# Attention scores of two key-tile pairs issued together as 64-row products

## The chip, the cores and the metric

The kernel runs on one core of a Trainium2 chip. The metric is the device time of one execution in microseconds, inputs and outputs in the chip's memory; the median of several executions is compared.

## The reference

There are 8 batches of 3136 tokens, a model width of 256, and a score width of 64. First comes an attention without softmax whose keys and queries are the same matrix, then a feed-forward block for the 128 tokens of each batch that score highest on a gate.

```python
scores = (1.0 / S) * np.matmul(z, z.transpose(0, 2, 1))      # z: 8 x 3136 x 64
attn = np.maximum(scores, 0.0) ** 2
x = u * np.matmul(attn, v)                                   # u, v: 8 x 3136 x 256
...
s = np.einsum('bsd,d->bs', x, w_gate)
top = np.argpartition(-s[b], capacity)[:capacity]            # capacity 128
h = np.maximum(x[b, top] @ w1, 0.0)
out[b, top] = x[b, top] + sigmoid(s[b, top]) * (h @ w2)      # w1: 256 x 1024, w2: 1024 x 256
```

All is float32. The scores are symmetric, since `z` stands on both sides.

## The kernel before

**Split operands.** Each float32 operand of the large products is split into a high part that TensorE's `float32r` type holds and a low part, the rest. `ZH` and `ZL` hold the two parts of the transposed `z` (64 rows), and each of the two tiles holds its 64 rows twice: in partitions 0 to 63 and again in 64 to 127. For a chunk of queries, `Z[b, c]` has the high part in rows 0 to 63 and the low part in rows 64 to 127. A product of 128 rows with `ZH` as the stationary operand therefore gives high by high plus high by low, and one with `ZL` gives low by high plus low by low: two matmuls for a key tile and a chunk of queries.

**Tiling.** The queries of a batch go in seven chunks (`CHUNKS`): five whole ones of 512 columns (`WHOLE` = 5), then one of 256 and one of 320. The keys go in 24 tiles of 128 and one half tile of 64. A slot (`slots`) is one chunk with two key tiles, or with the half tile; a chunk has 13 slots, twelve pairs and the half tile last. A pair is "old" (`is_old`) if its squared scores were already worked out for an earlier chunk as the other half of the symmetric matrix: they were transposed on VectorE (L453), stored to memory, and are fetched and only split again. Chunk `c` of the whole ones has 2c old pairs and 12 - 2c new ones; the chunks of 256 and 320 columns have 10 old and 2 new.

**Order of the slots.** Old and new pairs of a chunk are spread evenly over it by sorting on `(i + 0.5) / len`. The second new pair of a whole chunk (`is_second`, not in the very first chunk) works on 256 columns only, since the rest is the transpose of the first (`is_first`), and is put next to last among the new ones.

**One slot.** `mix(k)` issues the 12 products of a pair into two accumulators (L520): eight of the high part `hi` by `V`'s high and low part, then four of the low part `lo`. After the eighth it calls `between`, which issues the scores of slot k + 3 (`LEAD` = 3) by `scores(k)`. For a new pair that is four products into one of two score buffers (pool `ps_s`, `bufs=2`, each of two PSUM banks, one for each key tile of the pair), then on ScalarE a Relu (L424) and a Square that writes `hi` (L425), then on VectorE the product L435 of score and Relu, or on ScalarE a Square (L430), as a list of expected loads (`busy`) decides. `settle_scores` then issues L435 and `low`: the low part `lo` (L484, on GpSimd or VectorE), the transposes and the stores. A score buffer is free again when L435, or L424 where L430 is used, has read it.

**Other work.** TensorE executes in the order of the program, and each engine's order is written out by hand. Loads, splits of the next batch's `z` and `v`, fetches of old pairs and the routing are planned by slot number (`at_slot`) and run between the slots: routing multiplies with small stationary tiles (L721, L761, L771, L772, L844), spread over the slots of the next batch.

Of the kernel before, what the change touches and what calls it, by code (L numbers as in the profile page):

```python
# [10 lines left out]
F32 = mybir.dt.float32  # L11
# [7 lines left out]
P = 128  # L19
CH = 512  # L20
# [11 lines left out]
def chunks_of(S):  # L32

    n = (S - CH) // CH
    half = CH // 2
    rest = S - n * CH - half
    assert rest % Q == 0 and half <= rest <= CH
    return [(i * CH, CH) for i in range(n)] + [(n * CH, half), (n * CH + half, rest)]
# [46 lines left out]
def attention_then_routed_ffn(ctx: ExitStack, tc: tile.TileContext, zt, ut, v, wg, w1, w2, cst, cst16, keys, outs, at, cap):  # L85
    nc = tc.nc
# [4 lines left out]
    CHUNKS = chunks_of(S)  # L91
    NCH = len(CHUNKS)
    WHOLE = NCH - 2
# [16 lines left out]
    ps_s = ctx.enter_context(tc.tile_pool(name="ps_s", bufs=2, space=bass.MemoryType.PSUM))  # L110
# [76 lines left out]
    for o in range(0, W, 2 * D):  # L187
        kk, f = divmod(o, F)
# [6 lines left out]
    ZH = const.tile([P, S + 64], F32R, name="ZH")  # L195
    ZL = const.tile([P, S + 64], F32R, name="ZL")
# [3 lines left out]
    def by_rows(z, c0, n):  # L200

        g = c0 // CH * CH
        rows = slice((c0 - g) // P, (c0 - g + n) // P)
        return z[:, g : g + CH].rearrange("p (t f a) -> p f t a", t=GT, a=Q)[:, rows]

    Z = {}
# [97 lines left out]


    slots = []
    for b in range(B):
        for c in range(NCH):
            old = [(2 * g, 2 * g + 1) for g in range(min(c, WHOLE) * GT // 2)]
            new = [(2 * g, 2 * g + 1) for g in range(min(c, WHOLE) * GT // 2, NJ // 2)]  # L310
            if c < WHOLE and (b or c):

                new.insert(len(new) - 2, new.pop(1))
            both = [((i + 0.5) / len(old), 0, js, True) for i, js in enumerate(old)]
            both += [((i + 0.5) / len(new), 1, js, False) for i, js in enumerate(new)]
            slots += [(b, c, js, is_old) for _, _, js, is_old in sorted(both)]
            slots.append((b, c, (NJ,), False))
    assert len(slots) == B * NCH * SLOTS

# [16 lines left out]
    def is_second(k):  # L336

        b, c, js, _ = slots[k]
        return (b or c) and c < WHOLE and js[0] == c * GT + 2
# [6 lines left out]
    def spend(act=0.0, dve=0.0, pool=0.0):  # L346
        busy["act"] += act
        busy["dve"] += dve
        busy["pool"] += pool
# [35 lines left out]
    def old_scores(k):  # L385
        b, c, js, _ = slots[k]
        w = CHUNKS[c][1]
        g, t = js[0] // GT, js[0] % GT
        src = fetched[b, c, g][:, :, t * Q : (t + 2) * Q].rearrange("p f (q a) -> p q f a", a=Q)
        hi = work.tile([P, 2, CH], F32R, name="hi", tag="hi2", bufs=LEAD)[:, :, :w]  # L390
        by = lambda x: x.rearrange("p q (f a) -> p q f a", a=Q)
        nc.scalar.copy(by(hi), src)  # L392
        spend(act=0.15 + 0.00167 * w)
        lows.append((k, src, hi, [(by, src)], lambda: None))

    def turns(k):
        b, c, js, _ = slots[k]
        return c < WHOLE and js[0] * P >= CHUNKS[c][0] + CH

    def scores(k):  # L400
        b, c, js, is_old = slots[k]
        if is_old:
            return old_scores(k)
        n = len(js)
        c0, w = CHUNKS[c]
        mov = Z[b, c]
        if is_second(k):
            mov, w = mov.rearrange("p (f x) -> p f x", x=P)[:, :, P // 2 :], w // 2
        ps = ps_s.tile([P, 2, CH], F32, name="sc", tag="sc")[:, :, :w]
        todo = [(q, j, z) for q, j in enumerate(js) for z in (ZH, ZL)]  # L410
        if k < 2:
            todo.sort(key=lambda x: x[2] is ZL)
        for q, j, z in todo:
            nc.tensor.matmul(ps[:, q], z[:, j * P : (j + 1) * P], mov, start=z is ZH, stop=z is ZL)  # L414
        a = work.tile([P, 2, CH], F32, name="a", tag="a")[:, :n, :w]
        hi = work.tile([P, 2, CH], F32R, name="hi", tag="hi2", bufs=LEAD)[:, :n, : CHUNKS[c][1]]
        pieces = [(lambda x: x, a)]
        if is_second(k):
            by = lambda x: x.rearrange("p q (f x) -> p q f x", x=P)
            pieces = [(lambda x: by(x)[..., 64:], a.rearrange("p q (f x) -> p q f x", x=64))]  # L420
            pieces.append((lambda x: by(x)[..., :64], fetched[b, c, c].rearrange("p f (q x) -> p q f x", q=2)))
        act, dve = 0.13 + 0.0008 * w * n, 0.15 + 0.00104 * w * n
        turned = 0.16 + 0.00118 * w * n if turns(k) else 0.0
        nc.scalar.activation(a, ps[:, :n], AF.Relu)  # L424
        nc.scalar.activation(pieces[0][0](hi), pieces[0][1], AF.Square)  # L425
        for view, src in pieces[1:]:
            nc.scalar.copy(view(hi), src)
            spend(act=act)
        if n == 2 and busy["act"] + 3 * act < busy["dve"] + dve + turned:
            nc.scalar.activation(a, a, AF.Square)  # L430
            square = lambda: None
            spend(act=3 * act)
        else:
            rows = slice(0, P) if n == 2 else slice(64, P)
            square = lambda: nc.vector.tensor_tensor(a[rows], ps[rows, :n], a[rows], op=ALU.mult)  # L435
            spend(act=2 * act, dve=dve)
        lows.append((k, a, hi, pieces, square))
# [95 lines left out]
    rows = {}  # L533
# [590 lines left out]
    for b in range(B):  # L1124
        k0 = b * per

        for i in range(NCH):
            if b == 0:
                k = (0, 0, 0, 1, 3, 5, 6)[i]
            elif i < WHOLE:  # L1130
                k = k0 - per + (i + 1) * SLOTS + 7
            else:
                k = k0 - 1 + 4 * (i - WHOLE)
# [9 lines left out]
        for g in range(NJ // 2 + 1):  # L1143
            k = k0 - 10 + 3 * g // 2 if b else max(1, g - 2)
# [20 lines left out]
    for (b, c, g), ks in used.items():  # L1165
        k = max(ks[0] - AHEAD, room.popleft() - LEAD + 2)
# [6 lines left out]
    for i, (load, use) in enumerate(weight_tasks):  # L1173
        k = (1 + i // 4) * SLOTS
# [19 lines left out]
    def more_scores(upto):  # L1194
        nonlocal issued
        while issued <= min(upto, len(slots) - 1):
            scores(issued)
            issued += 1
# [199 lines left out]
```

## Time and profile before

| | |
|---|---|
| Median of 3 runs | 2113.93 us (2113.89 to 2115.18) |
| The profiled execution, and its span | 2112.39 us, 2110.6 us |
| Granted TensorE clock, mean | 0.998 |
| Busy share: PE, PEld, DVE, ACT, POOL | 99%, 83%, 72%, 60%, 64% |
| Matmuls, weight loads | 10583, 10583 |
| Chain by line, the two largest | PE acc L520 68%, PE sc L414 13% |

PE is TensorE's matmuls and PEld its weight loads, DVE is VectorE, ACT is ScalarE, POOL is GpSimd. The span runs from the first to the last instruction; the execution's time is a little longer. In a group of the profile, the shape `128*128 128x512` is a stationary tile of 128 rows and 128 columns and a moving operand of 128 rows and 512 columns. A matmul's own duration is a model, and matmuls overlap: what one costs is read from the start of one to the start of the next. In a timeline row the first number is the start in microseconds from the span's start, the second the time from the first start to the last end of the instructions merged in it; in brackets stands the idle time ahead of it, with what ended it. A row of waits has the work waited for, the microseconds in all, and how often.

### The profile page before, as it was taken

The page shows a single profiled execution, that of the slowest core. Times are in us where ns is not written, and L with a number is a line of the kernel's source. Part 1 is how long each engine was busy: PE and PEld are TensorE (multiplying, and loading weights), DVE is VectorE, ACT ScalarE, POOL GpSimd, SP SyncE. Part 2 cuts the span into 40 slices and gives each one's busy share as a digit, 9 for nine tenths or more (in the row PEclk, how much of TensorE's full clock was granted, in tenths as well). Part 3 has the DMA queues.
Part 4 walks back from the last instruction along what each step waited for, and adds up shares of the span by engine and source line. Part 5 has one row for each costly group of instructions (what it writes and reads, how often), then busy time and mean ns, then how long its engine had stood idle before and what let it go on. Part 6 is the DMA issues. An engine that isn't in the chain of part 4 may idle for free.

```text
span 2110.6 us, 31719 instructions
## 1 busy us (share of the span) xinstructions
PE 2091.1 (99%) x10583; PEld 1755.8 (83%) x10583; DVE 1529.9 (72%) x2304; ACT 1265.4 (60%) x1571; POOL 1347.7 (64%) x703
## 2 busy tenths in 40 slices
PE   8999999999999999999999999999999999999998
PEld 6788978889888898888988889888897888887788
DVE  8666678766777667776678766786667776787776
ACT  7565576545766457654676546765467654775543
POOL 6676577655766558765576655766567655666643
PEclk9999999999999999999999999999999999999999
DMA  6688766787667876678767787677775776665862
GB/s 187 198 250 231 201 187 172 187 231 215 180 185 183 230 206 188 190 187 226 212 185 190 185 225 209 187 199 184 208 229 174 196 189 169 201 186 160 215 175 93
DMA packets 425731, 412.03 MB, mean 195 GB/s; under 512 B 147616, under 2 KB 338912, under 8 KB 421984
## 3 DMA queue, kind: packets, MB, share of 16 engines
q1 hardware_dynamic: 424512, 407.66, 70.2%
q0 software_dynamic: 768, 2.10, 0.3%
q8 instruction: 83, 1.36, 0.3%
q14 instruction: 80, 0.66, 0.1%
q10 hardware_dynamic: 288, 0.26, 0.0%
HBM read 235.31 MB, written 172.23 MB: 193 GB/s over the span
## 4 chain that ended last, share of the span: by engine, by line
PE 83%; DMA 4%; DVE 4%; ACT 4%; issue 2%; POOL 2%; SPq 1%; POOLq 0%; DVEq 0%; ACTq 0%
PE acc L520 68%; PE sc L414 13%; DMA vst<-in_v 2%; ACT a L424 2%; POOL lo L484 1%; ACT hi L425 1%; DVE a L435 1%; DVE lo L484 1%; PE h L1038 1%; DMA squares<-aT 1%; DMA ut<-in_ut 0%; DMA qk<-squares_narrow 0%; PE y L1082 0%; DMA zst<-in_zt 0%; DVE ut L565 0%
## 5 line engine op out<-in xcount | busy, mean ns | idle before, releaser
L520 PE MATMUL acc<-hi,V 128*128 128x512 f32 (+2 forms) x5376 | 1230.6, 367 | 2.9 <-ACT hi L425 0.8
L484 POOL TENSOR_TENSOR lo<-a,hi 128x1024 fp32r<-128x1024 f32 (+2 forms) x327 | 756.5, 2316 | 609.5 <-DVE a L435 475.7
L520 PEld LDWEIGHTS acc<-hi,V 128*128 128x128 f32 x5376 | 932.5, 188 | 169.6 <-DVE ut L565 9.0
L520 PE MATMUL acc<-lo,V 128*128 128x512 f32 (+2 forms) x2688 | 666.2, 364 | 5.1 <-POOL lo L484 3.2
L424 ACT ACTIVATE a<-sc 128x1024 f32<-128x1024 f32 (+4 forms) x408 | 363.4, 891 | 507.1 <-PE sc L414 379.5
L520 PEld LDWEIGHTS acc<-lo,V 128*128 128x128 f32 x2688 | 473.8, 188 | 87.0 <-POOL lo L484 6.5
L435 DVE TENSOR_TENSOR a<-sc,a 128x1024 f32<-128x1024 f32 (+3 forms) x334 | 338.4, 1013 | 275.5 <-ACT hi L425 244.8
L392 ACT CAST hi<-qk 128x1024 fp32r<-128x1024 f32 (+2 forms) x320 | 275.0, 863 | 234.7 <-PE acc L520 205.2
L453 DVE STREAM_TRANSPOSE aT<-a 128x512 f32<-128x512 f32 (+1 forms) x520 | 340.9, 691 | 89.1 <-ACT a L430 61.9
L425 ACT ACTIVATE hi<-a 128x1024 fp32r<-128x1024 f32 (+4 forms) x408 | 377.4, 925 | 18.4 <-PE acc L520 1.1
L484 DVE TENSOR_TENSOR lo<-qk,hi 128x1024 fp32r<-128x1024 f32 (+2 forms) x223 | 308.9, 1393 | 66.5 <-ACT hi L392 63.4
L414 PE MATMUL sc<-Z,ZH 128*128 128x512 f32 (+2 forms) x760 | 281.4, 374 | 3.3 <-DVE a L435 2.2
L414 PE MATMUL sc<-Z,ZL 128*128 128x512 f32 (+2 forms) x760 | 278.7, 371 | 0.7 <-DVE ZL L120 0.7
L484 POOL TENSOR_TENSOR lo<-qk,hi 128x1024 fp32r<-128x1024 f32 (+2 forms) x97 | 190.3, 1964 | 56.9 <-ACT hi L392 37.8
L414 PEld LDWEIGHTS sc<-Z,ZH 128*128 128x128 f32 x760 | 142.9, 188 | 34.9 <-DVE a L435 8.0
L414 PEld LDWEIGHTS sc<-Z,ZL 128*128 128x128 f32 x760 | 142.9, 188 | 25.4 <-DVE ZL L120 1.1
L120 POOL TENSOR_TENSOR V<-vst,V 128x512 fp32r<-128x512 f32 x89 | 128.1, 1441 | 33.3 <-ACT V L119 33.0
L586 POOL TENSOR_TENSOR ut<-x,w_run 128x1024 f32<-128x1024 f32 (+2 forms) x52 | 127.0, 2442 | 23.3 <-DVE x L577 21.1
L119 ACT CAST V<-vst 128x512 fp32r<-128x512 f32 x95 | 57.8, 608 | 37.4 <-DMA vst<-in_v 37.4
L430 ACT ACTIVATE a<-a 128x1024 f32<-128x1024 f32 x74 | 78.6, 1062 | 2.3
L565 DVE SCALAR_TENSOR_TENSOR ut<-acc,ut 128x512 f32<-128x512 f32 (+2 forms) x112 | 64.0, 612 | 18.2 <-PE acc L520 17.9
L120 POOL TENSOR_TENSOR ZL<-zst,ZH 128x512 fp32r<-128x512 f32 (+2 forms) x56 | 73.6, 1320 | 3.0 <-DMA out<-x 2.2
(153 smaller groups left out, 1080.1 us busy)
## 6 DMA issues: line engine op xcount, KB each, us to landing
squares<-aT SPq DMA_DIRECT2D x160, 512.0 KB, 3.5
qk<-squares SPq DMA_DIRECT2D x320, 256.0 KB, 5.9
squares_narrow<-aT SPq DMA_DIRECT2D x320, 128.0 KB, 3.4
qk<-squares_narrow SPq DMA_DIRECT2D x80, 512.0 KB, 5.1
vst<-in_v SPq DMA_DIRECT2D x190, 128.0 KB, 3.2
out<-x SPq DMA_DIRECT2D x162, 128.0 KB, 3.3
ut<-in_ut SPq DMA_DIRECT2D x40, 512.0 KB, 4.6
squares_own<-aT SPq DMA_DIRECT2D x39, 256.0 KB, 2.1
```

Of the source, the lines that this page charges most:

```text
L120: (lo_on or nc.vector.tensor_tensor)(lo, src, hi.bitcast(F32), op=ALU.subtract)
L392: nc.scalar.copy(by(hi), src)
L414: nc.tensor.matmul(ps[:, q], z[:, j * P : (j + 1) * P], mov, start=z is ZH, stop=z is ZL)
L424: nc.scalar.activation(a, ps[:, :n], AF.Relu)
L425: nc.scalar.activation(pieces[0][0](hi), pieces[0][1], AF.Square)
L430: nc.scalar.activation(a, a, AF.Square)
L435: square = lambda: nc.vector.tensor_tensor(a[rows], ps[rows, :n], a[rows], op=ALU.mult)
L453: nc.vector.transpose(to, a[rows, q].rearrange("p (m t a) -> p m t a", t=GT, a=Q))
L484: on.tensor_tensor(view(lo), src, view(hi).bitcast(F32), op=ALU.subtract)
L520: nc.tensor.matmul(ac[h], w, mov, start=first and h not in started, stop=stop)
L565: nc.vector.scalar_tensor_tensor(xT[:, h, :w], acc[b, c][h], SCALE * SCALE, xT[:, h, :w], op0=ALU.mult, op1=ALU.mult)
L586: nc.gpsimd.tensor_tensor(wx, runs, consts["wg_run"].rearrange("p (o r) -> p o r", o=1).broadcast_to([P, NB, RUN]), op=ALU.mult,)
```

## The change

In whole chunks, new pairs now stand two and two in the list of slots (`units`; `paired` names the first of each two). The pair cut in half, what is left over, and in the very first chunk the first two pairs stay alone. When the scores of the first pair of a unit are due, `multiply` is called for both pairs, and `products` keeps the second's score buffer until its slot comes; Relu, Square and all that follows stay where the slot is. In a unit the products have 64 rows: one key tile of the pair works in rows 0 to 63, the other in rows 64 to 127 (`tile_position`), for three products each, high by high, high by low and low by high. The product low by low is left out. The moving operand is `Z` where it has the part in the right rows, and `ZH` or `ZL` itself, read through `by_rows` in runs of 32 columns, where it has not. Other new pairs have the products that they had.

```diff
+    paired = set()
...
-            if c < WHOLE and (b or c):
-                new.insert(len(new) - 2, new.pop(1))
...
+            units = [[js] for js in new]
+            if c < WHOLE:
+                second = [new.pop(1)] if b or c else []
+                lone = 0 if b or c else 2
+                units = [[js] for js in new[:lone]]
+                units += [new[i : i + 2] for i in range(lone, len(new), 2)]
+                if second:
+                    units.insert(len(units) - 1, second)
+            paired.update((b, c, u[0]) for u in units if len(u) == 2)
+            total, done = sum(map(len, units)), 0
+            both = [((i + 0.5) / len(old), 0, [js], True) for i, js in enumerate(old)]
+            for u in units:
+                both.append(((done + len(u) / 2) / total, 1, u, False))
+                done += len(u)
+            slots += [(b, c, js, is_old) for _, _, u, is_old in sorted(both) for js in u]
...
+    products = {}
+    def multiply(k):
+        b, c, js, is_old = slots[k]
+        c0, w = CHUNKS[c]
+        mov = Z[b, c]
...
+        ps = products[k] = ps_s.tile([P, 2, CH], F32, name="sc", tag="sc")[:, :, :w]
+        if (b, c, js) in paired or (k and slots[k - 1][:3] in paired):
+            low, high = slice(0, 64), slice(64, P)
+            zh = (mov[low], by_rows(ZH, c0, w)[high])
+            zl = (by_rows(ZL, c0, w)[low], mov[high])
+            for z, m in ((ZH, zh), (ZH, zl), (ZL, zh)):
+                for q, (j, rows) in enumerate(zip(js, (low, high))):
+                    nc.tensor.matmul(
+                        ps[:, q], z[rows, j * P : (j + 1) * P], m[q],
+                        start=m is zh and z is ZH, stop=z is ZL, tile_position=(rows.start, 0),
+                    )
+            return
...
     def scores(k):
...
+        if k not in products:
+            multiply(k)
+            if (b, c, js) in paired:
+                multiply(k + 1)
+        ps = products.pop(k)
```

More of the change, by code (lines that the diff above doesn't have):

```diff
@@ L310, in attention_then_routed_ffn @@
             new = [(2 * g, 2 * g + 1) for g in range(min(c, WHOLE) * GT // 2, NJ // 2)]
-            if c < WHOLE and (b or c):
-                new.insert(len(new) - 2, new.pop(1))
-            both = [((i + 0.5) / len(old), 0, js, True) for i, js in enumerate(old)]
-            both += [((i + 0.5) / len(new), 1, js, False) for i, js in enumerate(new)]
-            slots += [(b, c, js, is_old) for _, _, js, is_old in sorted(both)]
+            units = [[js] for js in new]
[13 more added lines that the diff above has]
+            slots += [(b, c, js, is_old) for _, _, u, is_old in sorted(both) for js in u]
             slots.append((b, c, (NJ,), False))
@@ L398, in turns @@
         return c < WHOLE and js[0] * P >= CHUNKS[c][0] + CH
+    products = {}
[3 more added lines that the diff above has]
+        mov = Z[b, c]
+        if is_second(k):
+            mov, w = mov.rearrange("p (f x) -> p f x", x=P)[:, :, P // 2 :], w // 2
+        ps = products[k] = ps_s.tile([P, 2, CH], F32, name="sc", tag="sc")[:, :, :w]
[10 more added lines that the diff above has]
+            return
+        todo = [(q, j, z) for q, j in enumerate(js) for z in (ZH, ZL)]
+        if k < 2:
+            todo.sort(key=lambda x: x[2] is ZL)
+        for q, j, z in todo:
+            nc.tensor.matmul(ps[:, q], z[:, j * P : (j + 1) * P], mov, start=z is ZH, stop=z is ZL)
     def scores(k):
@@ L404, in scores @@
         n = len(js)
[L405 to L414, printed above, removed]
+        w = CHUNKS[c][1] // (2 if is_second(k) else 1)
+        if k not in products:
[3 more added lines that the diff above has]
+        ps = products.pop(k)
         a = work.tile([P, 2, CH], F32, name="a", tag="a")[:, :n, :w]
```

## The prediction

> **What bounds the kernel now.** I read the page first: busy shares, the chain that ended last, then the groups by shape.
>
> ```profile
> span 2110.6 us, 31719 instructions
> PE 2091.1 (99%) x10583; PEld 1755.8 (83%) x10583; DVE 1529.9 (72%) x2304; ACT 1265.4 (60%) x1571; POOL 1347.7 (64%) x703
> PE 83%; DMA 4%; DVE 4%; ACT 4%; issue 2%; POOL 2%; SPq 1%; POOLq 0%; DVEq 0%; ACTq 0%
> L414 PE MATMUL sc<-Z,ZH 128*128 128x512 f32 x602 | 238.7, 397 | 3.3 <-DVE a L435 2.2 <-DVE Z L256 0.8
> L414 PE MATMUL sc<-Z,ZL 128*128 128x512 f32 x602 | 236.1, 393 | 0.7 <-DVE ZL L120 0.7
> ```
>
> PE is occupied for 99% of the span and is 83% of the chain; the next engine, DVE, has 72%. So PE's own stream sets the time: a matmul less is time less, and a wait of PE is time more. The scores with 512 columns are 602 + 602 matmuls, four for a pair of key tiles, so 301 pairs. The 397 ns of one is not what it costs, because matmuls overlap. The cost is the distance from start to start, which the timeline of PE shows:
>
> ```profile
> 403.77 0.39 PE L520 MATMUL acc<-lo,V 128*128 128x512 f32 x1
> 404.00 0.39 PE L414 MATMUL sc<-Z,ZH 128*128 128x512 f32 x1
> 404.22 0.39 PE L414 MATMUL sc<-Z,ZL 128*128 128x512 f32 x1
> 404.45 0.40 PE L414 MATMUL sc<-Z,ZH 128*128 128x512 f32 x1
> 404.69 0.39 PE L414 MATMUL sc<-Z,ZL 128*128 128x512 f32 x1
> 404.92 0.39 PE L520 MATMUL acc<-hi,V 128*128 128x512 f32 x1
> ```
>
> From 404.00 to 404.92 four score products take 0.92 us, 0.23 each.
>
> **The change part by part.** *Which slots.* From the code: every batch has, in its five whole chunks, 5, 4, 3, 2 and 1 units of two pairs (the pair cut in half by `is_second` and one more stay alone; the very first chunk also keeps two alone and still forms 5). That is 15 units a batch, 120 in all, 240 of the 301 pairs. Chunks of 256 and 320 columns are untouched.
>
> *Removed and added.* A unit now has 8 full-height products; after, 12 of 64 rows, which if they run two at a time are 6 steps. With 0.23 a step that is two steps less: 0.46 x 120 = 55 us as the gross gain. Matmuls and weight loads grow by 4 a unit, 480 each.
>
> *The switch between full-height and 64-row products.* Before, the kernel already has such places: routing multiplies with small stationary tiles. Around one of them, from narrow windows of PE's and of the weight loads' timeline:
>
> ```profile
> 391.12 0.39 PE L520 MATMUL acc<-lo,V 128*128 128x512 f32 x1
> 391.43 0.11 PEld L761 LDWEIGHTS <-mk 98*64 98x64 bf16 x1 [0.35 <-issue]
> 391.43 0.23 PE L761 MATMUL cols<-c,mk 98*64 98x98 bf16 x1
> 391.59 0.30 PEld L520 LDWEIGHTS acc<-hi,V 128*128 128x128 f32 x2
> 391.60 0.50 PE L520 MATMUL acc<-hi,V 128*128 128x512 f32 x1
> 391.94 0.64 PE L520 MATMUL acc<-hi,V 128*128 128x512 f32 x2
> ...
> 397.68 0.19 PE L771 MATMUL places<-mk,c 98*98 98x64 bf16 x1
> 397.81 0.12 PEld L772 LDWEIGHTS <-cs 64*98 64x98 bf16 x1 [0.22 <-issue]
> 397.81 0.23 PE L772 MATMUL places<-c,cs 64*98 64x64 bf16 x1
> 397.96 0.50 PE L520 MATMUL acc<-hi,V 128*128 128x512 f32 x1
> 398.30 0.62 PE L520 MATMUL acc<-hi,V 128*128 128x512 f32 x2
> ```
>
> Normally a weight load runs beside the matmul ahead of it (PEld overlaps PE). Here the load of the 64-column tile begins only at 391.43, 0.31 after the start of the last 512-column matmul, and the load for the way back at 391.59, not earlier. The same stands at 397.81 for a tile with 64 rows, the height of the change: its load is held back (0.22 of idle put down to "issue"), whereas L771 just ahead, with 98 rows and columns, starts without such a row. So going to 64 rows, and coming back, empties the array and lays the weight load bare. How long is the bare load? The second L520 after the switch starts at 391.94; the first cannot really have begun later than 391.94 - 0.23 = 391.71, so 0.12 after its load began. A switch behind a 512-column matmul thus takes 0.31 + 0.12 = 0.43 from start to start, in place of 0.23. I take the same for the way back; the short products above allow slightly less (397.81 to 398.30 - 0.23 = 398.07 is 0.26 for a whole 64-column product with its load and the switch).
>
> By this, a unit from the matmul ahead of it to the one behind it: now 9 x 0.227 = 2.04 us (0.227 lies between the 0.23 above and the 0.225 below); after, 0.43 + 5 x 0.227 + 0.43 = 2.00. So 0.05 less with rounding, times 120: -5 us (-8 to -3). The 55 us are nearly all eaten by the switches, two a unit.
>
> ```profile
> 397.23 0.62 PE L520 MATMUL acc<-lo,V 128*128 128x512 f32 x2
> ```
>
> (Two matmuls start between 397.23 and 397.68: 0.225 each.)
>
> *Do two 64-row products run side by side?* No row of this trace has two at once. The bounds: one step for two (6 steps, above), or one after another: 0.43 + 11 x 0.227 + 0.43 = 3.36, 1.32 x 120 = +158 us. I take one step for two, because the two work on disjoint rows of the array, and write different PSUM banks (`ps[:, 0]` and `ps[:, 1]` of 512 floats); the other end stays as a rival.
>
> *Do their weight loads run side by side?* Not shown either. A load alone takes the bare 0.12. One after the other, the second product begins 0.12 late, and a step lasts 2 x 0.12 = 0.24: 0.43 + 0.12 + 5 x 0.24 + 0.43 = 2.18, 0.14 x 120 = +17; with steps kept at 0.227, +9. For the sum I take loads side by side (-5), by the same disjoint rows, and give the other, +9 to +17, a chance of its own. The Trainium skill bears on this: "TensorE: Matmul & The Clock Gate", Part 3, draws the weight loads of four row tiles overlapping and their matmuls starting 4 ns apart, which would make it the -5; no run here shows it. "TensorEngine Tiling (Array Packing)", Key Properties, says that a change of the tiling mode drains the engine; the rows at 391.43 and 397.81 agree.
>
> *The buffers.* `ps_s` has two score buffers. Now the scores of slot k+3 are issued in the middle of slot k, and need the buffer that slot k+1's scores left: two slots for ScalarE's Relu and Square and VectorE's product L435. After, the second pair of a unit is issued about 0.9 us behind the first, a slot early, and needs the buffer of the scores just ahead of the unit. PE is in order: behind the waiting product stand the four low products of the same slot and all of the next, and no other engine can help. Where is there no slack? At the seams, where the single half tile (64 rows of `a`) comes right ahead of a unit. Batch to batch:
>
> ```profile
> 263.46 0.31 PE L414 MATMUL sc<-Z,ZH 128*128 128x320 f32 x1
> 264.36 3.74 DVE L484 TENSOR_TENSOR lo<-qk,hi 128x640 fp32r<-128x640 f32 x2
> 266.35 0.40 PE L414 MATMUL sc<-Z,ZH 128*128 128x512 f32 x1
> 267.87 0.75 PE L520 MATMUL acc<-hi,V 128*128 128x320 f32 x4
> 268.14 0.49 DVE L435 TENSOR_TENSOR a<-sc,a 64x320 f32<-64x320 f32 x1
> 268.69 0.50 PE L414 MATMUL sc<-Z,ZH 128*128 128x512 f32 x1
> ```
>
> The half tile scored at 263.46 is released at 268.14 + 0.49 = 268.63, since VectorE sat in two subtractions. Now PE starts the next-but-one scores at 268.69, just right. After, the unit starts at 266.35, its first pair is done by 266.35 + 0.2 + 3 x 0.23 = 267.24, and the second waits to 268.63: 1.4 us, less the idle that is there now (four 320-column products from 267.87: 0.75 less the 0.31 of the last is 0.44 for three steps, 0.147 each, so they are through by 268.46: 0.2): 1.2. Seven seams: 8. The next unit's second needs that one's buffer, which now also comes free on the dot; I put 0.4 x 7 = 3. First to second chunk:
>
> ```profile
> 311.35 0.39 PE L414 MATMUL sc<-Z,ZH 128*128 128x512 f32 x1
> 312.70 0.69 DVE L435 TENSOR_TENSOR a<-sc,a 64x512 f32<-64x512 f32 x1
> 314.08 0.39 PE L414 MATMUL sc<-Z,ZH 128*128 128x512 f32 x1
> ```
>
> Release at 313.39, 0.69 ahead of the use at 314.08; after, the use comes at 311.35 + 0.9 = 312.25: 1.1 us of wait, eight times: 9. In later chunks a stored pair stands between the half tile and the unit, and the slack was larger; I cost them at nothing, VectorE's idle being the cover. Sum 20 us. Against it, waits of the scores on VectorE that are there now would in part be the same ones:
>
> ```profile
>   DVE a L435: 10.2, 21
> ```
>
> (What the score line waited for: 10.2 us in 21 places, weight loads included.) I take 4 off: +16 us, between 0 (if the earlier Relu of the second pair shortens everything) and 28 (nothing taken off, and one more us a batch inside the first chunk).
>
> *The rest.* Instructions of ScalarE, VectorE, GpSimd and every DMA stay in number; stored pairs move by a slot or two, and with them the fetches planned from their slots. Reading the moving operand from `ZH`/`ZL` in runs of 32 columns costs nothing in my sum; the half tile (`is_second`) already reads in runs of 64, but runs of 32 are not shown (bounds 0 and +55, where a step would lose its gain).
>
> **The sum.** Span 2110.6 - 5 + 16 = 2122; with the 1.8 us around it (the profiled execution's 2112.39), 2123.4. The median 2113.93 is 1.5 above that execution: 2125.
>
> **The rivals.**
> A, loads in turn: +9 to +17 in place of -5, so 2114 + 12 + 16 = 2142. For it: a load of four-byte weights is long (0.12 of a step of 0.23), against: the rows are disjoint.
> B, no net wait for buffers: 2114 - 5 = 2109. For it: DVE is idle 28% of the span; against: at 264.36 to 268.63 it is not, and that work does not move.
> C, faster: the switch is cheap inside a busy stream, because loads for the other row half are fetched ahead. Then a unit is 7 x 0.227 = 1.59 to its successor, -54, and with +16 the time is 2076. It decides where both switches together cost less than 0.46 - 16 / 120 = 0.33 us; I read 0.40. Against it: the line of the 64-column tile has its idle put down to "issue" in all eight routings, 2.8 us together (the row below); for it: those tiles are 16-bit.
>
> ```profile
>   issue: 2.8, 8
> ```
>
> D, the change does not do what it says: 64-row products go one after another, +158; the second pair then comes 0.7 later, which halves the waits: 2114 + 158 + 8 = 2280. For it: nothing in the trace runs two at once.
>
> **How the numbers follow.** Forecast 2125 (own range 2113 to 2132): 0.44. A 0.22, B 0.14, C 0.09, D 0.11. The bound of no change is 0.2%, 4.2 us, about what a measurement here can tell. Faster: C and half of B, 0.17 with rounding. Same: the other half of B and the low end of the forecast, 0.14. Slower: the rest, 0.69. The range leaves out D and most of C and reaches over B and A: 2100 to 2148.
>
> **What would show it.** Right: matmul count up by 480; two score products starting within some ns, six distinct starts a pair; the first 64-row load about 0.31 behind the last full-height start, and again on the way back; PE's waits on "DVE a L435" up by some 16 us, at the seams. Wrong: starts of the two halves 0.12 apart (A) or 0.23 apart (D), loads running ahead across the switch (C), seams without a wait (B). What would upset it all is a slower step from the strided reads.

## The result and the profile after

The changed kernel takes 2142.11 us in the median (2138.65 to 2146.36, 4 runs), the one before 2113.91 beside it: a ratio of 1.0133, 95% interval 1.0112 to 1.0154. It is 28 us slower, where 11 were forecast. The direction was right, and waits for score buffers had been forecast; their size was not right, and the order of the slots had been costed at nothing. The profiled execution is the shortest of the four, 2138.65 us. Its page:

```profile
span 2136.9 us, 32777 instructions
PE 2091.3 (98%) x11063; PEld 1693.1 (79%) x11063; DVE 1547.5 (72%) x2291; ACT 1279.6 (60%) x1591; POOL 1326.4 (62%) x696
PE 78%; POOL 6%; DVE 6%; ACT 4%; issue 3%; DMA 3%; SPq 1%; POOLq 0%; ACTq 0%; DVEq 0%
```

Matmuls rose by 480 as worked out. PE's busy time is the same to 0.2 us, the span 26 us longer: by the profile all of the loss is time in which PE stood idle. In the chain PE fell from 83% to 78%. Line 426 holds the 64-row products, and what PE waited for stands in the table of waits (engine, line, what was waited for; microseconds in all, times, longest):

```profile
PE sc L426 <- DVE a L468: 14.0, 21, 1.7
PE acc L553 <- POOL lo L517: 9.0, 10, 2.1
PE sc L426 <- ACT a L457: 8.1, 7, 1.2
```

Before, the third was not there, and the first two were smaller:

```profile
PE sc L414 <- DVE a L435: 2.2, 4, 0.8
PE acc L520 <- POOL lo L484: 3.2, 2, 2.9
```

L468 is the old L435, L517 the old L484, L457 the old L424, L553 the old L520.

A unit in which nothing waits, in PE's timeline:

```profile
592.72 0.61 PE L553 MATMUL acc<-hi,V 128*128 128x512 f32 x2
593.26 0.50 PE L426 MATMUL sc<-Z,ZH 64*128 64x512 f32 x1
593.27 0.50 PE L426 MATMUL sc<-ZH 64*128 64x512 f32 x1
593.60 0.39 PE L426 MATMUL sc<-ZL,ZH 64*128 64x512 f32 x1
593.61 0.39 PE L426 MATMUL sc<-Z,ZH 64*128 64x512 f32 x1
593.84 0.39 PE L426 MATMUL sc<-ZH,ZL 64*128 64x512 f32 x1
593.84 0.39 PE L426 MATMUL sc<-Z,ZL 64*128 64x512 f32 x1
...
594.54 0.39 PE L426 MATMUL sc<-Z,ZL 64*128 64x512 f32 x1
594.54 0.39 PE L426 MATMUL sc<-ZH,ZL 64*128 64x512 f32 x1
594.86 0.50 PE L553 MATMUL acc<-lo,V 128*128 128x512 f32 x1
```

The two halves start within 0.01 us of each other, and a step is 0.23: they do run side by side, the strided reads (`sc<-ZH`, `sc<-ZL,ZH`) at the same pace. The first step alone is longer (593.26 to 593.60, 0.34), since the weight load lies bare: the recorded start of the first product must be some 0.11 ahead of its true start. The way back has 0.32 from 594.54 to 594.86 and the same bare load behind it. The weight loads beside it:

```profile
593.26 0.18 PEld L426 LDWEIGHTS sc<-Z,ZH 64*128 64x128 f32 x1 [0.35 <-issue]
593.27 0.18 PEld L426 LDWEIGHTS sc<-ZH 64*128 64x128 f32 x1
593.37 0.19 PEld L426 LDWEIGHTS sc<-ZL,ZH 64*128 64x128 f32 x1
593.38 0.19 PEld L426 LDWEIGHTS sc<-Z,ZH 64*128 64x128 f32 x1
```

The loads of the two halves also go side by side, 0.01 apart. The Trainium skill draws in "TensorE: Matmul & The Clock Gate", Part 3, overlapping weight loads and matmuls that start about 4 ns apart, for four row tiles. This trace agrees for two: the two products of a pair start within 10 ns of each other in 704 of the 720 pairs. The first load is held back by 0.35 just like the routing's.

And a unit that waits, in the same batch:

```profile
574.57 0.39 PE L553 MATMUL acc<-hi,V 128*128 128x512 f32 x1
574.88 0.50 PE L426 MATMUL sc<-Z,ZH 64*128 64x512 f32 x1
...
575.46 0.39 PE L426 MATMUL sc<-ZH,ZL 64*128 64x512 f32 x1
576.81 0.50 PE L426 MATMUL sc<-Z,ZH 64*128 64x512 f32 x1 [0.96 <-DVE a L468]
```

The first pair's last step starts at 575.46, the second pair's first step at 576.81 in place of 575.69: its buffer was still to be read by VectorE. Measured over all 120 units, from the start of the matmul ahead to the start of the second one behind, the median is 2.248 us and the mean 2.500. The mean excess, 0.252 x 120 = 30 us, is the whole loss and a little more. Of the 30, 1.5 are no wait: in the unit at 64.68, in the first batch, each step after the first takes 0.43 us in place of 0.23, and the granted clock between 64.0 and 66.5 is 0.60. (The trace of before has such a stretch, too: 0.68 between 60 and 70.) Some 29 us are waits.

### The profile page after: what moved, and what is told of

Read it like the earlier page. It is cut to its first block, busy times and chain, and to the rows that moved or that the text cites. A ratio compares the mean times of both kernels' runs of the same rounds, so it can differ in the third digit from the quotient of the medians.

```text
span 2136.9 us, 32777 instructions
## 1 busy us (share of the span) xinstructions
PE 2091.3 (98%) x11063; PEld 1693.1 (79%) x11063; DVE 1547.5 (72%) x2291; ACT 1279.6 (60%) x1591; POOL 1326.4 (62%) x696
## 4 chain that ended last, share of the span: by engine, by line
PE 78%; POOL 6%; DVE 6%; ACT 4%; issue 3%; DMA 3%; SPq 1%; POOLq 0%; ACTq 0%; DVEq 0%
PE acc L553 65%; PE sc L426 7%; POOL lo L517 4%; PE sc L435 4%; DVE a L468 2%; ACT hi L458 2%; ACT a L457 2%; POOL ut L619 1%; PE h L1071 1%; DMA vst<-in_v 1%; DMA squares<-aT 1%; DVE lo L517 1%; PE y L1115 1%; DVE aT L486 1%; DMA wl<-w2l_there 0%
## 5 line engine op out<-in xcount | busy, mean ns | idle before, releaser
L553 PE MATMUL acc<-hi,V 128*128 128x512 f32 (+2 forms) x5376 | 1232.1, 367 | 2.8 <-ACT hi L402 1.6
L517 POOL TENSOR_TENSOR lo<-a,hi 128x1024 fp32r<-128x1024 f32 (+2 forms) x327 | 743.2, 2279 | 604.4 <-DVE a L468 479.3
L553 PEld LDWEIGHTS acc<-hi,V 128*128 128x128 f32 x5376 | 928.3, 188 | 179.7 <-issue 15.3
L553 PE MATMUL acc<-lo,V 128*128 128x512 f32 (+2 forms) x2688 | 675.4, 368 | 10.1 <-POOL lo L517 9.0
L457 ACT ACTIVATE a<-sc 128x1024 f32<-128x1024 f32 (+4 forms) x408 | 362.0, 887 | 415.7 <-PE sc L426 139.4
L553 PEld LDWEIGHTS acc<-lo,V 128*128 128x128 f32 x2688 | 467.8, 188 | 113.7 <-issue 25.6
L468 DVE TENSOR_TENSOR a<-sc,a 128x1024 f32<-128x1024 f32 (+5 forms) x314 | 313.8, 999 | 231.0 <-ACT hi L458 213.9
L517 DVE TENSOR_TENSOR lo<-qk,hi 128x1024 fp32r<-128x1024 f32 (+2 forms) x230 | 342.5, 1498 | 102.5 <-ACT hi L402 101.2
L517 POOL TENSOR_TENSOR lo<-qk,hi 128x512 fp32r<-128x512 f32 (+2 forms) x90 | 179.0, 1993 | 80.4 <-ACT hi L402 56.4
L426 PE MATMUL sc<-Z,ZH 64*128 64x512 f32 x480 | 167.1, 426 | 22.3 <-DVE a L468 14.0
L426 PEld LDWEIGHTS sc<-Z,ZH 64*128 64x128 f32 x480 | 78.3, 185 | 76.9 <-issue 27.5
L426 PE MATMUL sc<-ZH 64*128 64x512 f32 x240 | 110.6, 461 | 0.0
L426 PE MATMUL sc<-ZL,ZH 64*128 64x512 f32 x240 | 94.8, 395 | 0.0
L426 PE MATMUL sc<-ZH,ZL 64*128 64x512 f32 x240 | 94.6, 394 | 0.0
L426 PE MATMUL sc<-Z,ZL 64*128 64x512 f32 x240 | 93.8, 391 | 0.0
L435 PE MATMUL sc<-Z,ZH 128*128 128x256 f32 (+2 forms) x280 | 90.5, 334 | 0.1
```

What stands on the lines that cost most here:

```text
L426: nc.tensor.matmul(ps[:, q], z[rows, j * P : (j + 1) * P], m[q], start=m is zh and z is ZH, stop=z is ZL, tile_position=(rows.start, 0),)
L517: on.tensor_tensor(view(lo), src, view(hi).bitcast(F32), op=ALU.subtract)
L553: nc.tensor.matmul(ac[h], w, mov, start=first and h not in started, stop=stop)
```

## The experiments

Theory 1: the time goes into waits of a unit's second pair for its score buffer. Theory 2: the 64-row products and their switches cost it. Theory 3: the order of the slots does. The kernel before ran beside each set; its medians there were 2114.6 us (the first four runs), 2115.4 (the next four) and 2113.5 (the last two).

**The order alone.** No 64-row branch, and no `multiply(k + 1)` in `scores`.

```diff
-            if (b, c, js) in paired:
-                multiply(k + 1)
...
-        if (b, c, js) in paired or (k and slots[k - 1][:3] in paired):
+        if False:
```

> The new order of slots alone: pairs stand two and two, but every pair's scores are issued in its own slot as four full-height products. Theory 1 (the time went into waits for score buffers, because the second pair of a unit asks for its buffer a slot early): no early asking, so about 2114, within 3 us of before. Theory 2 (the 64-row products and the switches of the array cost it): also about 2114. Theory 3 (the order itself disturbs VectorE, GpSimd and the fetches): most of the 28 us, 2130 to 2142.

Measured 2119.74 us, ratio 1.0023 (1.0013 to 1.0032): 5 us slower than before, and not the 28. Theory 3 falls, but the order is not free. Its waits on GpSimd's low part are those of the changed kernel (8.9 us in 11 places against 9.0 in 10), so that row belongs to the order:

```profile
PE acc L551 <- POOL lo L515: 8.9, 11, 2.8
```

Other short waits are new, too: in all, PE waits about 11 us longer in this trace than in that of before.

**Issued together, at full height.** Only the second of those two edits.

> New order, both pairs of a unit issued together, but as eight full-height products, so no switch of the array. Theory 1: the waits stay, and the 64-row products, worth about 3 us by the clean units of the changed kernel's trace, are gone: 2142 to 2148, at or a little above the changed kernel. The second pair's request comes 0.2 us later, which may take up to 0.2 x 35 = 7 us off. Theory 2: without switches the time falls back to about 2114.

Measured 2144.54 us, ratio 1.0151 (1.0134 to 1.0169). With not one 64-row product the loss is 30 us, as good as that of the changed kernel (the intervals overlap). Its table of waits has the same two rows, nearly the same size:

```profile
PE sc L435 <- DVE a L468: 13.0, 19, 1.5
PE sc L435 <- ACT a L457: 8.1, 7, 1.2
```

Issuing early adds 25 us to the 5 of the order, so the early issue makes most of the loss, and theory 2 falls. A clean unit of eight full-height products takes 2.315 us in this trace (median, from the matmul ahead to the second one behind), the clean 64-row unit 2.248: 0.07 less, 8 us in 120.

**64-row products, each pair in its own slot.** Only the first edit (no `multiply(k + 1)`).

> New order, 64-row products, but each pair of a unit issued in its own slot: 240 places with a switch there and back in place of 120, and no early request for a buffer. Theory 1 with the switch price read from the trace (0.43 us from start to start in, 0.43 out, 0.23 a step): 0.43 + 2 x 0.23 + 0.43 = 1.32 in place of 5 x 0.227 = 1.135, so +0.185 x 240 = +44, 2158. If switches cost nothing: 0.23 x 240 = 54 us less, 2060.

Measured 2153.47 us, ratio 1.0184 (1.0170 to 1.0198), 34 us over the run with the order alone. In its trace a slot with no wait takes 1.556 us from the matmul ahead to the second one behind, a full-height slot in the trace of before 1.373: 0.183 for each, where 0.185 was worked out, or 44 us for 240. A quarter of it does not reach the clock. Half of that stands in the table of waits, since a later PE no longer meets some that were there: on GpSimd's low part it waits 4.1 us here, and 8.9 with the order alone. Two switches for one pair cost more than the quarter of its products that they save.

```profile
PE acc L551 <- POOL lo L515: 4.1, 4, 2.7
```

**Score buffers strictly in turn.** In the second chunk's second unit the second pair did not wait for VectorE (586.12 below; the same in six batches, 1.44 us each by the excess of the unit):

```profile
585.04 1.02 ACT L457 ACTIVATE a<-sc 128x1024 f32<-128x1024 f32 x1 [1.26 <-DVE flip L773]
586.12 0.50 PE L426 MATMUL sc<-Z,ZH 64*128 64x512 f32 x1 [1.17 <-ACT a L457]
```

That Relu reads the scores of the unit's own first pair. In the built program both pairs of this unit are placed in the same score buffer. That is so for seven of the 120 units: this one in the second to the seventh batch, and one of the last batch's first chunk (the expectation below counts seven batches). The first pair's Square is ScalarE's, so that its buffer is free after the Relu, ahead of the older one, which VectorE was to read. That the scheduler gives a tile the buffer that it expects to be free first fits this, but was not looked into.

```diff
-    ps_s = ctx.enter_context(tc.tile_pool(name="ps_s", bufs=2, ...))
+    ps_s = ctx.enter_context(tc.tile_pool(name="ps_s", bufs=1, ...))
+    ps_t = ctx.enter_context(tc.tile_pool(name="ps_t", bufs=1, ...))
...
-        ps = products[k] = ps_s.tile(...)
+        turn_of[0] ^= 1
+        ps = products[k] = (ps_s, ps_t)[turn_of[0]].tile(...)
```

> The changed kernel, but the two score buffers are two pools of one buffer each, taken strictly in turn (before, whichever the scheduler expects free first: in the second unit of the second chunk it gave both pairs of a unit the same buffer, and the second waited 1.44 us for its partner's Relu, in seven batches). Theory 1: 7 x 1.4 = 10 us less than the changed kernel, about 2132. If that wait only moves to another place: about 2142.

Measured 2141.53 us, ratio 1.0116 (1.0098 to 1.0133): not told apart from the changed kernel. In its trace the six waits are gone; the unit of the last batch now waits for VectorE instead (1.3 us). But two other tiles, which I had left in one of the two pools, now waited for it near the end (1.7 us and 2.3 us on the rows `PE spread L680 <- DVE a L471` and `PE h L1074 <- ACT hr L1084`), and a batch's first unit waited some 1.4 us at four of the seven seams, where the changed kernel's did at one. So those two were put in turn, too:

> The changed kernel with the score buffers strictly in turn, as tried before, but now also for the other tiles that use these buffers near the end (gate scores and the expert's first layer), which had been put into one of the two and waited there for about 4 us. Theory 1: 7 waits of 1.4 us at the second chunk's second unit go, 2130 to 2136. If they move elsewhere: about 2142.

Measured 2136.05 us, ratio 1.0100 (1.0085 to 1.0114), 20.6 over before where the changed kernel is 28.2 over, at the upper edge of theory 1's range. The row on ACT a is gone, the one on VectorE has grown, since the first unit now waits at five of the seven seams:

```profile
PE sc L433 <- DVE a L475: 19.0, 23, 1.7
```

**Buffers free early.** For the slot two new slots ahead of a unit's second pair, half tiles too, ScalarE squares the Relu's result; its score buffer is then read by the Relu alone.

```diff
+    news = [k for k, s in enumerate(slots) if not s[3]]
+    early = {a for a, b in zip(news, news[2:]) if b and slots[b - 1][:3] in paired}
...
-        if n == 2 and busy["act"] + 3 * act < busy["dve"] + dve + turned:
-            nc.scalar.activation(a, a, AF.Square)
+        if k in early or n == 2 and busy["act"] + 3 * act < busy["dve"] + dve + turned:
+            rows = slice(0, P) if n == 2 else slice(64, P)
+            nc.scalar.activation(a[rows], a[rows], AF.Square)
```

> The changed kernel, but the score slot two new slots ahead of every unit's second pair (half tiles among them) has its Square on ScalarE (of the Relu's result) in place of VectorE's product, so that its buffer is free after the Relu alone; the products stay as they are. Theory 1 (the waits of a unit's second pair for its buffer cost about 30 us): nearly all of it comes back, 2114 to 2120, of which 5 over before are the order of the slots and -5 the 64-row products. Rival (the wait only moves, since ScalarE now is late for the next Relu and for hi): 2130 or more.

Measured 2134.97 us, ratio 1.0089 (1.0076 to 1.0103). A miss: some 9 us came back, not 25. Yet no unit waits for its buffer any more: what is left is 1.3 us at one unit of the first batch, for the low part `ZL` of `z`, and 1.8 at another, whose steps again take 0.43 us each. A new row stands at the head of the table, and the one on VectorE's low part has grown from 0.8:

```profile
PE acc L557 <- DVE ut L602: 12.5, 8, 1.8
PE acc L557 <- DVE lo L521: 5.5, 4, 3.3
```

Of the first, seven of the eight are at the starts of the batches. VectorE's timeline there:

```profile
275.43 1.30 DVE L490 STREAM_TRANSPOSE aT<-a 128x512 f32<-128x512 f32 x2 [1.07 <-ACT a L467]
276.66 1.78 DVE L521 TENSOR_TENSOR lo<-a,hi 128x1024 fp32r<-128x1024 f32 x1
278.36 0.88 DVE L602 SCALAR_TENSOR_TENSOR ut<-acc,ut 128x320 f32<-128x320 f32 x2
```

And PE's, which waits for the first of the two `ut`:

```profile
278.89 0.96 PE L557 MATMUL acc<-hi,V 128*128 128x512 f32 x3 [1.75 <-DVE ut L602]
```

The product `ut` reads the last accumulators of the batch before; PE needs one of them for the new batch. With VectorE rid of a product, the list of expected loads gave it a low part (1.78 us) that GpSimd had before, ahead of `ut`. The rival was right in kind (the wait moved), in another place than it named. The longest of the second row, 3.3 us at 17.3 in the first chunk, has no counterpart before; it waits for a low part on VectorE, too. At that place the granted clock is 0.5 for 3.4 us (17.2 to 20.6). In all, the five runs have a mean granted clock of 0.997 and the kernel before beside them 0.999, which by an estimate from these two figures is some 4 us of the 20 that are left.

**The same with full-height products**, to price the 64-row ones where units don't wait.

> As the run before this one (buffers free after the Relu), but with eight full-height products for a unit. The difference of the two is what the 64-row products with their two switches are worth where nothing waits: by clean units of the traces 2.29 us against 2.25 from the matmul ahead to the second one behind, 0.04 x 120 = 5 us more than the run before, 2119 to 2125. If 64-row products bring their full 0.46 a unit: 50 us more. If they cost: less.

Measured 2136.38 us, ratio 1.0097 (1.0082 to 1.0112): 1.4 us over the run with the 64-row products, with intervals that overlap. Its clean unit takes 2.315 us, not the 2.29 of the expectation, against 2.246: 8 us by the traces. These are neither confirmed nor excluded by the times; a gain of 50 is excluded.

**The old order, units where two new pairs are neighbours anyway**, buffers free early. The order is that of the kernel before, `early` is as above, and the units are chosen by this loop (`whole` is a new pair of 512 columns that is not cut):

```diff
+    k = 2
+    while k < len(slots) - 1:
+        if whole(slots[k]) and whole(slots[k + 1]) and slots[k][1] == slots[k + 1][1]:
+            paired.add(slots[k][:3])
+            k += 1
+        k += 1
```

> The order of the slots as before; units only where two new whole pairs are neighbours in it anyway (in the first three chunks, about 10 a batch), 64-row products there, and the Square on ScalarE as above so that buffers are free early. Theory 1: no cost of the order, about 85 units at -0.04: 2109 to 2113, at or just under before. If early requests still wait: 2115 to 2125.

Measured 2119.97 us, ratio 1.0027 (1.0016 to 1.0037), above the forecast. It has 80 units, not 85, and the same two rows at the head of its table:

```profile
PE acc L555 <- DVE ut L600: 12.7, 8, 1.8
PE acc L555 <- DVE lo L519: 5.8, 5, 3.3
```

That these are the reason is tried next.

**That low part back on GpSimd**, first with the old order (and no units in the very first chunk, which leaves 75), then with the changed kernel's.

```diff
+                if b and c == 0 and js[0] == 4:
+                    on, took = nc.gpsimd, 0.1 + 0.0021 * of
                 on.tensor_tensor(view(lo), src, view(hi).bitcast(F32), op=ALU.subtract)
```

> The old order with units where two new pairs are neighbours (80, none in the very first chunk) and buffers free early, and for the second pair of each batch's first unit the low part L484 on GpSimd, as it was before; in the run with the old order the list of loads had moved it to VectorE, ahead of the ut product that frees the accumulator, and PE waited 1.75 us for that in seven batches. Theory 1 (each wait has a place of its own, and these 12 us and 3 us of the first chunk go): 2103 to 2108 where before is 2114. Rival (VectorE and GpSimd bound the seam, so the wait comes back elsewhere): 2112 to 2120.

Measured 2112.76 us, ratio 0.9996 (0.9987 to 1.0005): level with the kernel before, where the run before it was 4.6 us over: 5 us came back, and not the 15 that were forecast. The waits on `ut` are gone (0.3 us left), and so is the one of 3.3 us in the first chunk. The time lies in the rival's range, but not for the rival's reason: at the first four seams (from 262 to 280, and in three more such stretches, 69 us in all) PE is busy for 68.9, and just ahead of them it waits little more than before (for VectorE's low part 3.1 us in 5 places, against 1.8 in 3). New short waits of the 64-row line took part of the gain, six of 0.7 us by the excess of the unit, behind a split of `z` that the low part now precedes on GpSimd:

```profile
PE acc L557 <- DVE ut L602: 0.3, 1, 0.3
PE sc L427 <- POOL ZL L120: 2.7, 6, 0.5
```

> The changed kernel's order with all 120 units and buffers free early, and the same low part on GpSimd: against the run with early buffers (2135), 7 x 1.75 = 12 us less, 2121 to 2125; what is then left over before is the order of the slots (5 us when alone) and the first chunk of all. Rival: 2130 or more.

Measured 2126.04 us, ratio 1.0049 (1.0036 to 1.0063): 1 us above the forecast, and 12.6 over before where the run with VectorE's low part was 19.6 over: 7 us came back. With no wait left for a score buffer at its units, the change is still slower than before. The units still lose 5.8 us to waits for `ZL`, 0.7 in each of six batches and 1.5 in the first batch:

```profile
PE sc L429 <- POOL ZL L120: 2.7, 6, 0.5
```

Its table has waits on the low parts besides (8.9 us on GpSimd, 5.1 on VectorE, against 3.2 and 1.8 before); the order alone has the first of the two, and 3.3 us of the second are again the place in the first chunk.

## Why the prediction fell short

**The switch and the step: right.** A unit was worked out at 0.43 + 5 x 0.227 + 0.43 from the routing's rows. The clean unit has 0.32 + 0.11, steps of 0.23, and 0.32 + 0.11 back. Against a full-height unit put together from before's slots (1.373 + 4 x 0.229 = 2.289 to the second matmul behind) its 2.248 are 0.04 less, 5 us in 120, the term of the forecast; against the full-height units that ran, 2.315, they are 0.07 less, 8 us, the end of its range. Halves side by side (rival D falls), loads side by side (rival A's mechanism falls, though its time, 2142, is the measured one: a number that fits is no proof). Rival C falls: the load does not run ahead across the switch. Rival B falls: there was a net wait. One count is off without harm to the sum: the 602 products with `ZH` hold those of 40 half tiles, so there are 281 pairs of 512 columns, not 301, of which 240 are in units.

**The step that failed is the sum of the waits for buffers, +16.** It was mis-sized: measured at the units, by place, it is 29:

- Seams between batches: 8 + 3 forecast; 2.2 at a batch's first unit and 4.8 at its second in the profiled execution. The first unit's wait comes and goes: it is 1.36 us at one of the seven seams in this trace, some 0.3 at four and nothing at two (these two are 0.14 shorter than the median unit, since the products around them have 320 columns), while the runs with buffers in turn have it at four and five of seven. That is up to 7 us from one execution to the next, and may be why the runs of this kernel spread over 8 us; this was not tested.
- First to second chunk: 9 forecast, 6.4 measured.
- The second chunk's second unit: nothing forecast. The sum has a second unit's wait at the seams between batches alone; the words on a stored pair and VectorE's idle are for the first units of later chunks, and those did not wait. Measured 8.6, in six batches: both pairs of the unit had the same buffer. The forecast took for granted that the two buffers are used in turn. With them in turn these waits go, and the kernel is some 8 us faster (the intervals just touch), though the seams then wait more often.
- The first chunk of the last batch: nothing forecast, 1.4 measured, by the same fault.
- The first chunk of the first batch: nothing forecast for its units, 5.2 measured. I had looked for seams, and this chunk has tight spots of its own while the inputs still come in.
- "I take 4 off", for waits that were there before: the 10.2 us that it was taken from count weight loads. PE's own waits on `DVE a` were 2.2 us, and 1.1 of them, in the first chunk, are there in the changed kernel as well, so that 1.1 at most could be taken off.

**The order of the slots was costed at nothing; alone it costs 5 us** (an interval of 3 to 7). A wait of 0.53 us on GpSimd's low part in six batches, and one of 1.8 in the first, are part of it; how much each of the other short waits in its table counts on the clock is open.

The sum, from one run to the next: +5 for the order, +25 for issuing early, -2 for the 64-row products (not told apart from 0 or from -8) make the 28 measured. By the traces the waits at the units are 29 and the products -5 to -8; that the first shows as 25 on the clock is not explained.

**What the forecast did not see and the runs showed** is the next limit. Early buffers removed the units' waits and gave back only 9 us, because VectorE's `ut` then ended last at the start of a batch, behind a low part that the list of expected loads had moved there. With that low part on GpSimd another 7 us came back, and other waits of the units appeared, for `ZL`. A long wait can also go with a lower clock: in the four traces that wait 3 us for a low part in the first chunk (all with buffers free early), the granted clock is 0.5 for 3.4 to 6.8 us at that place, and in none of the others. Why is not shown.

## What to carry to other kernels

Running two 64-row products side by side halves their time, but each change between full-height and 64-row products empties the array and lays a weight load bare: price two switches from a place in the trace where the kernel already makes them, and set that against the steps saved; here about 0.4 of 0.46 us went. Work pulled together to share a switch asks for its buffers earlier, on an engine that runs in order, so for every place list which buffer it takes, who still has to read it, and when; a scheduler that picks the buffer may not take them in turn. Where an engine is busy for 99%, price a new order of the work as well: a wait of half a microsecond that returns in six batches is 3 us.

## What was not expected of the hardware

The bare weight load costs two halves no more than one: four loads start in pairs 0.01 us apart (593.26, 593.27, then 593.37, 593.38), and the first step is 0.34 in place of 0.23, once and not twice. And moving operands read in runs of 32 columns keep the step of 0.23, as contiguous ones do.
